# A new layout for the turned attention weights, and earlier quarter sums, in a fused threshold-attention and GELU-MLP kernel

## The chip, the cores and the metric

The kernel runs on one core of one Trainium2 chip. Its time is device microseconds from the first instruction to the last. Five engines work side by side and meet only at semaphores: TensorE (PE in the profile; its weight loads are PEld), VectorE (DVE), ScalarE (ACT), GpSimd (POOL) and SyncE (SP, which here only issues transfers). Sixteen DMA engines move data between HBM and SBUF and within SBUF.

## The reference, cut to what matters

```python
# threshold attention: 8 batches x 8 heads, 576 tokens, head size 64
scores = scale * np.matmul(q, k.transpose(0, 1, 3, 2))
thresh = np.max(scores, axis=-1, keepdims=True) - tau
scores = np.where(scores >= thresh, scores, -1000000000.0)
scores = scores - np.max(scores, axis=-1, keepdims=True)
attn = np.exp(scores)
attn = attn / (np.sum(attn, axis=-1, keepdims=True) + 1e-09)
attn_out = np.matmul(attn, v).astype(np.float32)
# bridge (B,H,S,D) -> (B*S, H*D) = (4608, 512), then the MLP, 512 -> 2048 -> 512
x = np.ascontiguousarray(attn_out.transpose(0, 2, 1, 3)).reshape(B * S, H * D)
h = x @ w_in
g = 0.5 * h * (1.0 + erf(h * inv_sqrt2))      # exact GELU
return (g @ w_out).astype(np.float32)
```

`q`, `k`, `v` are float32; `w_in` and `w_out` arrive as 8-byte floats, which the kernel turns into float32 itself ("conversions" below).

## The kernel before

Two heads make a pair; there are 32 pairs, each in five slots of 128 query rows (the fifth slot holds the 64 left-over rows of both heads). The program is one long list in which every engine's instructions stand in order. Three stages follow one another:

1. **Start** (the first four pairs, some 20 slots). The MLP weights are read and converted; attention weights are turned (queries to the free axis) by TensorE.
2. **Middle** (pairs 4 to 31). The attention weights are turned by VectorE in blocks of 32 x 32, and transfers within SBUF put the blocks in their places (the "regrouping"). TensorE fills the room between with ten of the eighteen MLP blocks of 256 tokens.
3. **End** (the last eight blocks, two at a time, by a Strassen-like scheme with seven products instead of eight). It needs sums and differences of quarters of `w_in` and of the blocks' inputs.

The tiles and the turning, with cuts:

```python
pd = [const.tile([P, 4 * KR, P], FP32, name=f"pd{e}") for e in range(2)]     # P=128, KR=5, Q=32, NB=18
...
def turn_p(p, i):                      # VectorE, in the middle stage: one operation for each head
    w = s.pop(("p", i))
    n = 1 if i == NC else 2
    for e in reversed(range(n)):
        to = pd_tail[p % 2] if i == NC else pd[e][:, :, i * Q:(i + 1) * Q]
        nc.vector.transpose(to[:, 0:NB, :], w[:, e * S:(e + 1) * S].rearrange("p (b i) -> p b i", i=Q))

def regroup(p, i):                     # SyncE issues; i = 1 and 3 move two slots at once, i = NC the tail
    if i == 1:
        s["pT"] = [one.tile([P, KR, S], FP32, tag=f"pT{e}", name=f"pT{e}") for e in range(2)]
    for a in range(4):
        rows = slice(a * Q, (a + 1) * Q)
        if i == NC:
            e, at = divmod(a * Q, TAIL)
            nc.sync.dma_start(s["pT"][e][:, :, MAIN + at:MAIN + at + Q], pd_tail[p % 2][rows])
            continue
        half = slice((i - 1) * Q, (i + 1) * Q)
        for e in (1, 0):
            nc.sync.dma_start(s["pT"][e][:, :, a * P:(a + 1) * P][:, :, half], pd[e][rows, :, half])

def weigh_v(p, lo, hi):                # called twice a pair, with halves of 288 columns
    for c in range(KR):
        for e in range(2):
            nc.tensor.matmul(xT[f, 0:hi - lo], lhsT=s["v"][:, e, c, :], rhs=pT[:, c, lo:hi], ...)
```

A row of `pT` is (5, 576): one matmul reads 288 numbers in a row, and one transfer writes runs of 64 numbers, 256 bytes.

The first loads, and the change from the middle to the end:

```python
def load_early(p):                     # q and k of the first four pairs; v in the same way
    ... src[b, 2 * hp + e, 0:MAIN, :].rearrange("(t p) d -> p t d", p=P)   # runs of 64 numbers
...
elif n == len(slots):
    ext = weights_in()                 # s1, s2, s4: twelve sums of w_in's quarters, on VectorE
...                                    # two slots later: the last pair's weigh_v, then its division
fill(1e12, B * S)                      # what is left of the plain MLP blocks
strassen(*ext)

def strassen(ext, room):
    for h in range(HF // U):
        for c in range(NK):
            a = w_in_sb[c][:, HF + h * U:HF + (h + 1) * U]
            vec.tensor_tensor(a, w_in_sb[c][:, h * U:(h + 1) * U], a, op=ALU.subtract)
    ...
    x_sums(*DUOS[0])                   # four differences of the first two blocks' quarters
    for sb, (n1, n2) in enumerate(DUOS):
        for j in range(NJ):
            product(x, [(lhs_in(c, j, 0), a[:, c, :]) for c in ks], True)
            product(y, [(lhs_in(c, j, 1), b[:, c, :]) for c in ks], True)
            product(x, [(lhs_ext(s2, c, j), t2[:, c, :]) for c in ks])
            ...
        for m in ms:                   # the last products of a duo
            product(xs[m], rows(g12, m, w_out_part(1, 1)))
            nc.scalar.copy(lo[m][:, HD:2 * HD], xs[m])
            row = n1 * TOK + m * P
            nc.sync.dma_start(out[row:row + P, :], lo[m])
```

`lhs_in(c, j, 1)` reads the half of `w_in` that the loop at the head of `strassen` overwrites. `t1`, `t2`, `t4` are what `x_sums` writes.

Of the kernel before, what the change touches and what calls it, by code (L numbers as in the profile page):

```python
# [18 lines left out]
def kernel(  # L19
# [68 lines left out]
    ps = ctx.enter_context(tc.tile_pool(name="ps", bufs=4, space=PSUM))  # L88

    ident = const.tile([P, P], FP32, name="ident")  # L90
    make_identity(nc, ident)
# [3 lines left out]
    v_sb = [const.tile([P, 2, KR, D], FP32, name=f"v{i}") for i in range(4)]  # L95
    pd = [const.tile([P, 4 * KR, P], FP32, name=f"pd{e}") for e in range(2)]
    sums = [const.tile([P, Q], FP32, name=f"sums{i}") for i in range(2)]
# [3 lines left out]
    for t in q_tail + v_sb:  # L101
        nc.gpsimd.memset(t, 0.0)
    for t in pd:
        nc.gpsimd.memset(t[:, NB:4 * KR, :], 0.0)

# [31 lines left out]
    def load_piece():  # L137
        if loaded[0] == len(pieces):
            return
        dst, src = pieces[loaded[0]]  # L140
        loaded[0] += 1
        if not wide:
            nc.sync.dma_start(dst, src)
            converted[0] += 1
            load_piece()
            return
        k = loaded[0] - 1
        if k % 2:

            room = pd[k // 2 % 2][:, 0:NB - 2, :].bitcast(U32).rearrange("p b i -> p (b i)")  # L150
            raw, shifted = room[:, 0:2 * PIECE], room[:, 2 * PIECE:4 * PIECE]
        else:
            raw, shifted = (xg.tile([P, 2 * PIECE], U32, tag="x", name=s) for s in ("raw", "shifted"))
        nc.gpsimd.dma_start(raw, src.bitcast(U32))
        n = 8 * PIECE - 4
        nc.gpsimd.dma_start(shifted.bitcast(U8)[:, 0:n], src.bitcast(U8)[:, 3:3 + n])
        raws.append((dst, raw, shifted))
# [78 lines left out]
    def load_early(p):  # L236
        b, hp = divmod(p, HP)
        s = st[p] = {}
        for name, src in (("q", q), ("k", k)):
            t = s[name] = ld.tile([P, NC + 1, P], FP32, tag=name, name=name)  # L240
            eng = nc.scalar if p < 2 and name == "k" else nc.sync
            for e in range(2):
                eng.dma_start(
                    t[:, 0:NC, e * D:(e + 1) * D],
                    src[b, 2 * hp + e, 0:MAIN, :].rearrange("(t p) d -> p t d", p=P),
                )
            eng.dma_start(
                t[0:TAIL, NC, :].rearrange("p (e d) -> p e d", e=2),
                src[b, 2 * hp:2 * hp + 2, MAIN:S, :].rearrange("e s d -> s e d"),
            )  # L250

    def load_v_early(p):
        b, hp = divmod(p, HP)
        t = st[p]["v"] = v_sb[p % 4]
        for e in range(2):
            nc.sync.dma_start(t[:, e, 0:NC, :], v[b, 2 * hp + e, 0:MAIN, :].rearrange("(t p) d -> p t d", p=P))
            nc.sync.dma_start(t[e * TAIL:(e + 1) * TAIL, e, NC, :], v[b, 2 * hp + e, MAIN:S, :])
# [165 lines left out]
    def turn_p(p, i):  # L423

        s = st[p]
        w = s.pop(("p", i))
        n = 1 if i == NC else 2  # L430
        for e in reversed(range(n)):
            to = pd_tail[p % 2] if i == NC else pd[e][:, :, i * Q:(i + 1) * Q]
            nc.vector.transpose(to[:, 0:NB, :], w[:, e * S:(e + 1) * S].rearrange("p (b i) -> p b i", i=Q))  # L433

    def regroup(p, i):

        s = st[p]
        if i == 1:
            s["pT"] = [one.tile([P, KR, S], FP32, tag=f"pT{e}", name=f"pT{e}") for e in range(2)]
        for a in range(4):  # L440
            rows = slice(a * Q, (a + 1) * Q)
            if i == NC:
                e, at = divmod(a * Q, TAIL)
                nc.sync.dma_start(s["pT"][e][:, :, MAIN + at:MAIN + at + Q], pd_tail[p % 2][rows])
                continue
            half = slice((i - 1) * Q, (i + 1) * Q)
            for e in (1, 0):
                nc.sync.dma_start(s["pT"][e][:, :, a * P:(a + 1) * P][:, :, half], pd[e][rows, :, half])

    def weigh_v(p, lo, hi):  # L450
# [5 lines left out]
        for c in range(KR):  # L456
            for e in range(2):
                f = slice(e * D, (e + 1) * D)
                pT = s["pT"][0 if p < EARLY and c == NC else e]
                nc.tensor.matmul(  # L460
                    xT[f, 0:hi - lo], lhsT=s["v"][:, e, c, :], rhs=pT[:, c, lo:hi],
                    start=(c == 0), stop=(c == KR - 1))
        by = None if p < EARLY else s["inv"]
# [27 lines left out]
    dirty = [False]  # L491
    warm = const.tile([P, 2], FP32, name="warm")
    nc.vector.memset(warm, 0.0)

    def gelus(left):
# [14 lines left out]
    def block_steps(n):  # L510

        g = {}
        for j in range(N_DF):
            if j % 2 == 0:
# [10 lines left out]
        for m in range(TOK // P):  # L525
            for j in range(N_DF):
                yield NS_OUT, len(pieces) - N_DF + j + 1
                if j not in g:
# [9 lines left out]

    mlp = {"n": 0, "steps": None, "next": None, "debt": 0.0}

# [40 lines left out]
    def weights_in():  # L581

        room = [x for tag in ("q", "k", "qT", "kT") for _ in range(2) for x in unit(ld, tag)]
        room += unit(work, "p", 2) + unit(work, "p", 2)
        rest = [units(v_sb[i % 4])[0] for i in range(NP - 4, NP - 1)]
        s1, s2, s4 = ({} for _ in range(3))
        for h in range(HF // U):
            lo, hi = slice(h * U, (h + 1) * U), slice(HF + h * U, HF + (h + 1) * U)
            for c in range(NK):
# [4 lines left out]
                vec.tensor_tensor(s4[c, h], w_in_sb[NK + c][:, lo], s2[c, h], op=ALU.subtract)  # L594
        return (s1, s2, s4), room + rest

# [9 lines left out]

    def strassen(ext, room):
        s1, s2, s4 = ext
        for h in range(HF // U):
            for c in range(NK):  # L610
                a = w_in_sb[c][:, HF + h * U:HF + (h + 1) * U]
                vec.tensor_tensor(a, w_in_sb[c][:, h * U:(h + 1) * U], a, op=ALU.subtract)
        room = room + units(v_sb[(NP - 1) % 4]) + [u for t in pd_tail for u in units(t)]
        room += [x for _ in range(2) for x in unit(xg, "x", 2)]
        x_ext = [room.pop().rearrange("p (c t) -> p c t", c=NK) for _ in range(3)]
        o_ext = [room.pop() for _ in range(2)]
        room += [x for _ in range(N_DF // 2 + 2) for x in unit(gp, "g")]
        room += [u for t in pd for u in units(t)]
        for e in range(2):
# [28 lines left out]

        def x_sums(n1, n2):
            t1, t2, t4 = x_ext  # L650
            a, b = x_blk[n1], x_blk[n2]
            b11, b21, b12, b22 = a[:, 0:NK, :], a[:, NK:2 * NK, :], b[:, 0:NK, :], b[:, NK:2 * NK, :]
            vec.tensor_tensor(t1, b12, b11, op=ALU.subtract)
            vec.tensor_tensor(t2, b22, t1, op=ALU.subtract)
            vec.tensor_tensor(b12, b22, b12, op=ALU.subtract)  # L655
            vec.tensor_tensor(t4, b21, t2, op=ALU.subtract)

        def w_out_sums(j):
# [5 lines left out]
            vec.tensor_tensor(wt4(j), b21, wt2(j), op=ALU.subtract)  # L664

        def finish_chunk(j, x, p3):
            product(x, p3)
# [4 lines left out]

        x_sums(*DUOS[0])
        for sb, (n1, n2) in enumerate(DUOS):
# [45 lines left out]
            for m in ms:  # L720
                xs[m] = bank("sc")[:, 0:HD]
                product(xs[m], rows(g11, m, w_out_part(0, 0)), True)
                nc.scalar.copy(lo[m][:, 0:HD], xs[m])
                vec.tensor_tensor(lo[m][:, 0:HD], lo[m][:, 0:HD], vs[m], op=ALU.add)
            for n in DUOS[sb + 1] if sb + 1 < len(DUOS) else ():
                if n in away:
                    bring(n)
            if sb + 1 < len(DUOS):
                x_sums(*DUOS[sb + 1])
            for m in ms:  # L730
# [6 lines left out]
            for m in ms:  # L737
                product(ys[m], rows(g22, m, wt4))
                vec.tensor_tensor(hi[m][:, 0:HD], hi[m][:, 0:HD], ys[m], op=ALU.add)
            for m in ms:  # L740
                product(xs[m], rows(gs1, m, wt1))
                vec.tensor_tensor(hi[m][:, HD:2 * HD], hi[m][:, HD:2 * HD], xs[m], op=ALU.add)
                row = n2 * TOK + m * P
                nc.sync.dma_start(out[row:row + P, :], hi[m])
            for m in ms:
                product(xs[m], rows(g12, m, w_out_part(1, 1)))
                nc.scalar.copy(lo[m][:, HD:2 * HD], xs[m])
                row = n1 * TOK + m * P
                nc.sync.dma_start(out[row:row + P, :], lo[m])

    load_early(0)
    load_early(1)
    for _ in range(2):
# [8 lines left out]
    for g, (chunks, pairs) in enumerate(parts):  # L762
        first = 0 if g < 2 else HP + g - 2
        slots += [(p, i) for p in range(first, first + pairs) for i in chunks]
    BATCH = HP * SLOTS
    WEIGH = 2
    START = 2 * HP + 2
# [17 lines left out]
    for n in range(len(slots) + WEIGH + 1):  # L785
# [15 lines left out]
        if p > EARLY and i == WEIGH:  # L801
            made = [weigh_v(p - 1, h * HALF, (h + 1) * HALF) for h in range(2)]
        owed += (goal(n) - goal(n - 1)) * BLK_NS * (PARTS[i] if not early and p < NP else 1.0)
# [33 lines left out]
        if n == BATCH:  # L837
            for t in pd_tail:
                nc.gpsimd.memset(t[:, NB:4 * KR, :], 0.0)
# [61 lines left out]
```

## Time and profile before

| | value |
|---|---|
| time, median of 3 runs (lowest, highest) | 1428.99 us (1428.49, 1430.3) |
| profiled span | 1430.0 us |
| TensorE busy / weight loads busy | 1385.1 / 960.9 us |
| VectorE / ScalarE / GpSimd busy | 900.0 / 640.8 / 389.1 us |
| packets on the queues of SyncE (q1) | 423184, of 449492 in all |
| `pT<-pd` transfers | 448 of 160 KB, median 3.9 us to landing |
| VectorE turning, `pd<-p` 128x576 | 224 of 756 ns, 160.8 us |

How to read it: busy time is the union of an engine's instructions, and matmuls are pipelined, so a busy TensorE isn't TensorE at its peak; the distance from one matmul's start to the next one's says more. An engine that is not the limit costs nothing while it waits. In the waits view, "A <- B: total, times, longest" says that A sat idle until B had finished. In the timeline a row is start, length, engine, line, operation, names, count, with the idle time before it in brackets. `o_ps`, `hT` are the plain MLP, `bank` the end stage, `sc` the scores, `xT` the product with `v`, `tr` TensorE's turning.

### The profile page before, as it was taken

The numbers are of one execution on the slowest core, as the hardware profiler recorded it, in microseconds if no ns is written. First come the engines' busy times: TensorE is split into PE (matmuls) and PEld (weight loads), VectorE is DVE, ScalarE is ACT, GpSimd is POOL, SyncE is SP. The second block draws the span as 40 slices with busy tenths as digits, with TensorE's granted clock in tenths as the row PEclk, the third lists the DMA queues.
The fourth block names the chain that finished last, engine by engine and source line by source line (L and its number), as shares of the span: only waits on it lengthen the run. The fifth ranks groups of instructions, "written<-read, shape, count | busy, mean of one in ns | idle before, by whom it ended". The sixth has DMA issues, their size and how long they took to land.

```text
span 1430.0 us, 19776 instructions
## 1 busy us (share of the span) xinstructions
PE 1385.1 (97%) x6544; PEld 960.9 (67%) x6544; DVE 900.0 (63%) x1908; ACT 640.8 (45%) x1039; POOL 389.1 (27%) x810
## 2 busy tenths in 40 slices
PE   5898999999999999999999999999999999999999
PEld 4666547566466574665746657466488888888887
DVE  5887787777767777777777777777654142241230
ACT  5758525436256373562745627457142141230320
POOL 4443244433434434434434344330000000000000
PEclk8999999999999999999999999999999999999999
DMA  9977167776667776677776777765500100100000
GB/s 260 297 264 241 40 144 150 152 150 133 131 137 145 153 147 133 142 140 159 156 140 143 160 154 152 142 135 100 107 0 1 44 1 0 59 1 8 22 1 30
DMA packets 449492, 167.06 MB, mean 117 GB/s; under 512 B 413040, under 2 KB 432048, under 8 KB 449392
## 3 DMA queue, kind: packets, MB, share of 16 engines
q1 hardware_dynamic: 423184, 108.65, 38.8%
q0 software_dynamic: 23808, 56.57, 12.9%
q8 instruction: 53, 0.87, 0.2%
q10 hardware_dynamic: 2400, 0.59, 0.2%
q14 instruction: 47, 0.39, 0.1%
HBM read 71.68 MB, written 11.47 MB: 58 GB/s over the span
## 4 chain that ended last, share of the span: by engine, by line
PE 85%; DVE 6%; ACT 5%; DMA 2%; issue 1%; SPq 1%; POOL 0%; DVEq 0%; ACTq 0%; POOLq 0%
PE bank L641 27%; PE hT L520 18%; PE o_ps L532 17%; PE sc L355 12%; PE xT L460 9%; ACT p L370 2%; DVE p L386 1%; PE tr L301 1%; DVE nmx L367 1%; DVE power L185 1%; ACT L500 1%; ACT diag L400 1%; DMA pd<-in_moe_w_in_dram 1%; ACT L507 0%; DVE expo L176 0%
## 5 line engine op out<-in xcount | busy, mean ns | idle before, releaser
L370 ACT ACTIVATE p<-sc,nmx 128x576 f32<-128x576 f32 x288 | 202.5, 739 | 384.4 <-DVE nmx L367 384.4
L367 DVE TENSOR_REDUCE nmx<-sc 128x1 f32<-128x576 f32 x288 | 205.0, 749 | 149.8 <-PE sc L355 149.8
L520 PE MATMUL hT<-x,w_in 128*128 128x256 f32 x1280 | 296.2, 384 | 0.0
L532 PE MATMUL o_ps<-w_out,g 128*128 128x512 f32 x640 | 295.1, 604 | 0.0
L520 PEld LDWEIGHTS hT<-x,w_in 128*128 128x128 f32 x1280 | 238.4, 190 | 56.9 <-issue 25.2
L386 DVE SCALAR_TENSOR_TENSOR p<-sc,thr,p 128x576 f32<-128x576 f32 x288 | 225.4, 816 | 65.2 <-ACT p L370 64.2
L368 POOL TENSOR_SCALAR thr<-nmx,tau_eff 128x1 f32<-128x1 f32 x288 | 85.0, 295 | 547.4 <-DVE nmx L367 544.9
L532 PEld LDWEIGHTS o_ps<-w_out,g 128*128 128x128 f32 x640 | 117.1, 190 | 141.0 <-issue 139.2
L355 PE MATMUL sc<-kT,qT 64*128 64x288 f32 x960 | 165.0, 432 | 2.6 <-DVE p L386 2.4
L460 PE MATMUL xT<-pT,v 128*64 128x288 f32 (+2 forms) x1280 | 164.4, 409 | 3.2 <-ACT g L500 3.2
L433 DVE STREAM_TRANSPOSE pd<-p 128x576 f32<-128x576 f32 x224 | 160.8, 756 | 2.9
L355 PEld LDWEIGHTS sc<-kT,qT 64*128 64x128 f32 x960 | 92.9, 187 | 84.2 <-issue 71.8
L460 PEld LDWEIGHTS xT<-pT,v 128*64 128x64 f32 x1280 | 90.2, 137 | 73.4 <-issue 13.5
L232 POOL DMA_DIRECT2D v<-in_v_dram x208 | 111.0, 537 | 10.5 <-issue 9.5
L641 PE MATMUL bank<-x,w_in 128*128 128x256 f32 x384 | 94.7, 383 | 3.2 <-DVE x L655 3.2
L507 ACT ACT_TABLE_LOAD x71 | 91.1, 1283 | 1.3
L500 ACT ACT_TABLE_LOAD x71 | 91.1, 1283 | 1.3
L641 PE MATMUL bank<-unit 128*128 128x256 f32 x352 | 88.6, 382 | 0.0
L641 PEld LDWEIGHTS bank<-x,w_in 128*128 128x128 f32 x384 | 73.7, 192 | 14.2 <-issue 4.1
L223 POOL DMA_DIRECT2D q<-in_q_dram x104 | 70.9, 686 | 15.9 <-issue 15.0
L641 PEld LDWEIGHTS bank<-unit 128*128 128x128 f32 x352 | 67.4, 192 | 9.4
L301 PE MATMUL tr<-diag,p 128*128 128x128 f32 (+1 forms) x360 | 51.8, 312 | 22.1 <-ACT diag L400 13.8
(143 smaller groups left out, 1346.4 us busy)
## 6 DMA issues: line engine op xcount, KB each, us to landing
pT<-pd SPq DMA_DIRECT2D x448, 160.0 KB, 3.9
pT<-pd_tail SPq DMA_DIRECT2D x112, 80.0 KB, 2.8
q<-in_q_dram POOLq DMA_DIRECT2D x104, 72.0 KB, 4.0
k<-in_k_dram POOLq DMA_DIRECT2D x104, 72.0 KB, 2.6
out_dram<-o_sb SPq DMA_DIRECT2D x28, 256.0 KB, 3.9
inv<-turned SPq DMA_DIRECT2D x56, 128.0 KB, 3.9
v<-in_v_dram POOLq DMA_DIRECT2D x156, 40.0 KB, 3.0
raw<-in_moe_w_in_dram POOLq DMA_DIRECT2D x8, 512.0 KB, 5.5
```

The source lines that it names most:

```text
L232: eng.dma_start(t[r:P:4, e, 0:n, :], rows[:, r * KR:r * KR + n, :])
L355: nc.tensor.matmul(sc[e][:, h, 0:HALF], lhsT=lhsT, rhs=s["kT"][rows, at:at + HALF], start=True, stop=True)
L367: nc.vector.tensor_reduce(nmx[:, e:e + 1], sc, axis=AXIS.XY, op=ALU.max, negate=True)
L370: nc.scalar.activation(w[:, e * S:(e + 1) * S].rearrange("p (h s) -> p h s", h=2), sc, AF.Exp, bias=nmx[:, e:e + 1], scale=1.0)
L386: nc.vector.scalar_tensor_tensor(row, sc[e][:, :, 0:HALF], thr[:, e:e + 1], row, op0=ALU.is_ge, op1=ALU.mult, accum_out=den[e])
L433: nc.vector.transpose(to[:, 0:NB, :], w[:, e * S:(e + 1) * S].rearrange("p (b i) -> p b i", i=Q))
L460: nc.tensor.matmul(xT[f, 0:hi - lo], lhsT=s["v"][:, e, c, :], rhs=pT[:, c, lo:hi], start=(c == 0), stop=(c == KR - 1))
L500: nc.scalar.activation(t, hT, AF.Gelu)
L507: nc.scalar.activation(warm[:, 1:2], warm[:, 0:1], AF.Exp)
L520: nc.tensor.matmul(hT[:, j % 2, :], lhsT=w_in_sb[c][:, j * P:(j + 1) * P], rhs=x_blk[n][:, c, :], start=(c == 0), stop=(c == N_DM - 1))
L532: nc.tensor.matmul(o[:, 0:d_model], lhsT=g[j][:, m * P:(m + 1) * P], rhs=w_out_sb[j], start=(j == 0), stop=(j == N_DF - 1))
L641: nc.tensor.matmul(to, lhsT=l, rhs=r, start=start and k == 0, stop=k == len(pairs) - 1, skip_group_check=not start)
```

## The change

**Turned weights.** One tile `turned_p` of shape (2 heads, 2 halves, 20, 64) for each partition takes the place of the two `pd`. One VectorE operation turns both heads of a slot. `pT` is read as (9 groups of 64 queries, 5, 64), so that one regrouping transfer writes 128 runs of 5 x 64 numbers, 1280 bytes. The product with `v` then reads its columns as groups of 64, 320 numbers apart, and is split in 320 and 256 columns instead of 288 and 288.

**End stage.** The differences within `w_in` and the first `x_sums` are put behind the last slot, into `weights_in`, two slots ahead of the last division. Each output row block is stored in two halves, each as soon as it is complete.

**Start.** `k` and `v` of the first four pairs are read with four rows of HBM next to each other in a partition (runs of 1024 bytes); `q` stays as it was. A first Exp on a dummy tile stands behind the first loads. The zeros in the padding of the turned weights are written when the middle stage begins, no longer at the very start.

```diff
-    pd = [const.tile([P, 4 * KR, P], FP32, name=f"pd{e}") for e in range(2)]
+    turned_p = const.tile([P, 2, 2, 4 * KR, 2 * Q], FP32, name="turned_p")
+    pd = [turned_p[:, e, :, :, :].rearrange("p h b i -> p (h b i)") for e in range(2)]
...
-    for t in pd:
-        nc.gpsimd.memset(t[:, NB:4 * KR, :], 0.0)
...
+                order = "(t p) d -> p t d" if name == "q" else "(p t) d -> p t d"
                 eng.dma_start(
+                    t[:, 0:NC, e * D:(e + 1) * D], src[b, 2 * hp + e, 0:MAIN, :].rearrange(order, p=P))
...   # turn_p
-        for e in reversed(range(n)):
-            to = pd_tail[p % 2] if i == NC else pd[e][:, :, i * Q:(i + 1) * Q]
-            nc.vector.transpose(to[:, 0:NB, :], w[:, e * S:(e + 1) * S].rearrange("p (b i) -> p b i", i=Q))
+        nc.vector.transpose(
+            turned_p[:, :, i // 2, 0:NB, i % 2 * Q:(i % 2 + 1) * Q], w.rearrange("p (e b i) -> p e b i", e=2, i=Q))
+
+    def by_64(t):
+        return t.rearrange("p c s -> p (c s)").rearrange("p (g c s) -> p g c s", c=KR, s=2 * Q)
...   # regroup
-                nc.sync.dma_start(s["pT"][e][:, :, a * P:(a + 1) * P][:, :, half], pd[e][rows, :, half])
+                nc.sync.dma_start(by_64(s["pT"][e])[:, 2 * a + h, :, :], turned_p[rows, e, h, :, :])
...   # weigh_v
+                    to = to.rearrange("p (g s) -> p g s", s=2 * Q)
+                    rhs = by_64(s["pT"][e])[:, lo // (2 * Q):hi // (2 * Q), c, :]
...   # weights_in, behind the twelve sums
+        for h in range(HF // U):
             for c in range(NK):
                 a = w_in_sb[c][:, HF + h * U:HF + (h + 1) * U]
                 vec.tensor_tensor(a, w_in_sb[c][:, h * U:(h + 1) * U], a, op=ALU.subtract)
+        x_sums(x_ext, *DUOS[0])
...   # strassen
-        x_sums(*DUOS[0])
...
+                store(n2, m, hi[m], 0)
...
-                row = n1 * TOK + m * P
-                nc.sync.dma_start(out[row:row + P, :], lo[m])
+                store(n1, m, lo[m], HD)
...
     load_early(0)
+    nc.scalar.activation(warm[:, 1:2], warm[:, 0:1], AF.Exp)
     load_early(1)
...
+    WIDE = 5 * 2 * Q
...
-            made = [weigh_v(p - 1, h * HALF, (h + 1) * HALF) for h in range(2)]
+            made = [weigh_v(p - 1, lo, hi) for lo, hi in ((0, WIDE), (WIDE, S))]
...
-            for t in pd_tail:
+            for t in pd_tail + [turned_p[:, e, h, :, :] for e in range(2) for h in range(2)]:
                 nc.gpsimd.memset(t[:, NB:4 * KR, :], 0.0)
```

## The prediction, made before the changed kernel ran

> **What bounds the kernel now.** I read the busy shares by slice first, then a table of the stages, then TensorE's own waits, and last the timeline around the one long wait late in the run.
>
> ```profile
> PE 1385.1 (97%) x6544; PEld 960.9 (67%) x6544; DVE 900.0 (63%) x1908; ACT 640.8 (45%) x1039; POOL 389.1 (27%) x810
> ...
> PEclk8999999999999999999999999999999999999999
> ```
>
> TensorE is busy almost everywhere. The stage table says where it isn't; its columns are the window, its length, each engine's busy us with counts, granted clock, DMA share, GB/s.
>
> ```profile
> 0.00:200.00 200.00, 168.40 (x932) 116.99 (x932) 150.67 (x335) 127.26 (x235) 77.54 (x168) 0.93 0.73 213
> 200.00:1000.00 800.00, 795.37 (x3711) 487.90 (x3712) 605.14 (x1239) 408.94 (x542) 310.64 (x639) 1.00 0.71 143
> 1000.00:1040.00 40.00, 36.77 (x131) 19.19 (x128) 23.08 (x44) 5.70 (x9) 0.88 (x3) 0.92 0.48 95
> 1040.00:1430.00 390.00, 384.58 (x1777) 336.86 (x1775) 121.10 (x292) 98.88 (x254) 0.00 (x0) 1.00 0.04 15
> ```
>
> In the 800 us of the middle TensorE lacks 4.6 us, at full clock. VectorE (76%) and the DMA engines (71%) have room there. So the start lacks 31.6 us, the passage to the end stage 3.2 us, the end 5.4 us. That no slack hides in this busy time I took from the distances of starts in the trace: between 200 and 1015 us the plain MLP's matmuls of 256 columns start a median 216 ns apart, the same as in the end stage, where nothing else runs.
>
> ```profile
> PE tr L301 <- ACT diag L400: 13.8, 7, 5.6
> PE tr L275 <- DMA q<-in_q_dram: 6.5, 1, 6.5
> ...
> PE xT L460 <- ACT g L500: 3.2, 2, 1.6
> PE bank L641 <- DVE x L655: 3.2, 1, 3.2
> ...
> PE sc L355 <- DVE p L386: 2.4, 7, 1.0
> ...
> PE tr L283 <- DMA q<-in_q_dram: 1.8, 1, 1.8
> ```
>
> No wait for `pT`, for a regrouping or for the turning (L433) is in TensorE's list. What the change is named for is off the path; its side parts touch the waits that exist.
>
> ```profile
> 1029.13 0.95 DVE L478 TENSOR_TENSOR x<-xT,inv 128x64 f32<-128x64 f32 x4 [5.30 <-DMA inv<-turned]
> ...
> 1030.00 2.49 DVE L612 TENSOR_TENSOR w_in<-w_in 128x512 f32<-128x512 f32 x4
> ...
> 1030.31 1.03 PE L641 MATMUL bank<-x,w_in 128*128 128x256 f32 x4
> ...
> 1033.73 0.68 DVE L655 TENSOR_TENSOR x<-x 128x512 f32<-128x512 f32 x1
> ...
> 1034.57 2.04 PE L641 MATMUL bank<-x,w_in 128*128 128x256 f32 x4 [3.23 <-DVE x L655]
> ...
> 1036.40 1.91 PE L641 MATMUL bank<-unit 128*128 128x256 f32 x4
> ...
> 1040.89 1.03 PE L641 MATMUL bank<-unit 128*128 128x256 f32 x4
> ```
>
> Here the first product of the end stage runs at 1030.31, and the second waits until VectorE, itself held 5.30 us by `inv`, has divided, differenced `w_in` and made the first `x_sums`. The same four matmuls then take 2.04 us instead of 1.03: half clock, until 1040.
>
> **What the skill says.** (1) "TensorE: Matmul & The Clock Gate", part 1, the HAM clock gate: an idle window of about 3.4 us puts the array at half clock, and a busy one brings it back. The trace agrees: 3.23 us idle, then some 5.3 us with starts 427 ns apart instead of 216. (2) "VectorE: DVE Perf Modes", the errata section: an fp32 tensor_tensor takes (N+151)/0.96 ns; at N=576 that is 757, and the turning measures 756 here, so I use it for the merged one. (3) "DMA: Bandwidth & Descriptors", why small descriptors are slow: it says that transfers within SBUF suffer little. The trace's packets of 256 bytes from HBM in the start took 18 ns each, of 4096 bytes 159 ns or more: 14 against 26 bytes per ns. (4) "Advanced Engine Details and Errata", SBUF cachelines: full rate needs consecutive accesses in one 16-byte line. Runs of 64 floats meet that. No run so far shows a matmul with such a stepped operand.
>
> **The change, part by part.**
>
> *Turning.* 28 pairs x 4 slots x 2 = 224 operations of 756 ns become 112 of (1152+151)/0.96 = 1357 ns (estimate): 112 x (1512 - 1357) = 17 us of VectorE. TensorE's waits on VectorE in the middle are the seven of `sc <- p L386`, 2.4 us. I grant 0.7 us.
>
> *Regrouping.* 448 transfers go from 640 runs of 256 bytes to 128 of 1280: some 230,000 of 423,184 packets vanish. TensorE waits for none, so this is 0 us on the path. SyncE's issue of one (median 0.9 us) may shorten too, also hidden.
>
> *Product with v.* 320 + 256 columns are the 576 of before, in as many instructions: 0 us, if the stepped operand costs nothing.
>
> *Passage.* VectorE's list behind the last slot: the twelve sums end at 1023.83; then four differences (2.5 us) and four `x_sums` (4 x 0.69 = 2.7 us) end near 1029.0, inside the 5.30 us in which it waited for `inv` anyway. The second product needs nothing later, so TensorE goes on at 1031.2. Removed: a start distance of 3.61 us instead of 0.22, so 3.4 us; and 13 matmuls at half clock, with the first of them slow too, 2.8 us. Together **6.2 us**; I count 5.9, for a bank that might come free late.
>
> *Start.* The first wait, 6.49 us, ends with the first `q`; up to 7 us about 3,650 packets of 256 bytes went by in the trace's packet records, 2,170 of them `k` on ScalarE's queue. As a quarter as many of 1024 bytes, at an estimated 48 ns (between 18 for 256 and 159 for 4096), `k` takes 1.6 instead of 2.4 us of the sixteen engines, and the Exp's table load (1.28 us) delays the second `k` behind it: 0.7 us gained. The table load itself, at 6.42 us, hid behind TensorE's turning of `k`, so it's worth some 0.1 more. From 10 to 60 us the DMA engines are full, and the conversions wait for them; VectorE serves conversions and attention in one order, so that the 5.6 us wait at 22.35 us goes back to weights that landed at 20.8 us. `k` and `v` of the four pairs are 8 x 1,024 = 8,192 packets; 2,048 of those are the first two `k`. The other 6,144 cost 6,144 x 18 / 16 = 6.9 us of the engines, and 1,536 x 48 / 16 = 4.6 us in the new form: 2.3 us, of which I take 1.7 to reach TensorE. GpSimd issues the first weights 0.56 us earlier without its two zero fills; those were converted without a wait, so 0. The 200 us of the start lose 7% of the clock, 14 us, beside 31.6 us idle; with 2.5 us less idle I count 0.5 less of it. Sum of the start **3.0 us**. TensorE is saturated from 200 us on, so what the start gains arrives at the end whole.
>
> *Tail.* The last transfer is 128 KB instead of 256 KB; at the 26 bytes per ns and engine of above that is 0.3 us less.
>
> Sum: 0.7 + 5.9 + 3.0 + 0.3 = 9.9 us, 1428.99 - 9.9 = **1419 us**.
>
> **Rivals.** *A: the stepped operand slows the product with v.* xT takes 5.0 us a pair (a timeline row of 40 such instructions is 5.07 us long), 28 x 5.0 = 140 us in all. A quarter slower would be +35 us: 1454. For it speaks only that no such operand has been seen here; against it, point (4). I give 4%. *B: the start eats its gain.* Its waits pass between `diag`, gelu and DMA (5.0 us on L500 alone), and the 93% clock there shifts with each gap; in-order lists can catch the gain at the next gelu. Then only passage and tail remain: 1422. *C: the other way, the start gains more than traffic:* fewer gaps, so less half clock; of the 14 us of clock loss some 3 us more could come back, and some of the 5.6 us wait: 1415. *D: the passage's wait moves,* for the last division or a free bank: 2 to 3 us given back, 1422.
>
> **Range and chances.** B and D pull up by 3 us each, C down by 3 or 4; from 1419 this makes 1412 to 1424.5. Faster by over 2% would need 28.6 us, nearly all that the start loses: 2%. Slower by over 2% is rival A alone: 4%. The rest, 94%, is within 2%.
>
> **What would show each step.** Right: no wait of TensorE of over 1 us near 1030 us, and the four-matmul rows there at 1.03 us; a first matmul at about 5.7 us; turning operations of 1152 columns near 1357 ns; q1 packets near 190,000; middle windows with busy and starts as before. Wrong: xT starts over 240 ns apart for each two instructions (rival A); a start stage with over 31 us idle (B); the half clock back at the passage (D).

## The result, and the profile after

| | before | after |
|---|---|---|
| time, median (lowest, highest) | 1429.19 (1428.49, 1430.3) | 1422.57 us (1420.38, 1423.59) |
| ratio, 95% interval | | 0.9951 (0.9934 to 0.9968) |
| profiled span | 1430.0 | 1421.8 us |

The change saves about 7 us, 0.5%: within the 2% band, inside the predicted range, 3.6 us above the predicted time. The same changed kernel was timed a second time among the experiments (-6.1 us). The two profiles that are compared below lie 8.2 us apart: the profile of the kernel before is of an execution of 1432.1 us, slower than the four timed ones, so the differences between the two profiles are somewhat larger than those between medians.

First the page of the changed kernel: busy times, packets, and the groups that the change touches.

```profile
PE 1382.1 (97%) x6544; PEld 958.8 (67%) x6544; DVE 892.6 (63%) x1788; ACT 640.9 (45%) x1040; POOL 388.0 (27%) x812
...
DMA packets 219347, 167.05 MB, mean 117 GB/s; under 512 B 122480, under 2 KB 203952, under 8 KB 219248
...
q1 hardware_dynamic: 193040, 108.65, 36.2%
...
q10 hardware_dynamic: 2400, 0.59, 0.2%
...
L473 PE MATMUL xT<-pT,v 128*64 128x256 f32 (+1 forms) x1280 | 163.7, 409 | 2.7 <-ACT g L509 2.7
L434 DVE STREAM_TRANSPOSE turned_p<-p 128x1152 f32<-128x1152 f32 x112 | 154.1, 1376 | 3.0
```

SyncE's queue q1 lost 230,144 packets, as counted. The merged turning takes 1376 ns; 1357 was the estimate. The product with `v` keeps its busy time (164.4 us before). In q10, ScalarE's queue with the first `k`, the 2400 packets are the same number as before: the transfers that were to be made of fewer, longer packets were not.

The stage table after, with the same windows and columns:

```profile
0.00:200.00 200.00, 169.73 (x934) 117.39 (x936) 150.66 (x330) 127.47 (x236) 77.94 (x170) 0.94 0.71 214
200.00:1000.00 800.00, 795.71 (x3718) 488.23 (x3718) 598.99 (x1128) 408.88 (x542) 309.22 (x639) 1.00 0.66 143
1000.00:1040.00 40.00, 40.00 (x159) 23.32 (x155) 26.42 (x51) 9.23 (x18) 0.87 (x3) 1.00 0.45 95
```

The last window is full now, at full clock, where 3.2 us were missing. The middle has 0.3 us more TensorE time, and its DMA share fell from 0.71 to 0.66. The start has 1.3 us less idle time, but only 0.4 us of it shows in the starts of matching instructions (below).

TensorE's own waits after:

```profile
PE tr L302 <- ACT diag L401: 11.4, 7, 2.8
PE tr L276 <- DMA q<-in_q_dram: 9.5, 2, 6.3
PE tr L302 <- ACT g L509: 5.0, 4, 2.3
PE xT L473 <- ACT g L509: 2.7, 2, 1.3
PE sc L356 <- DVE p L387: 2.5, 6, 0.9
```

The wait of the end stage for `x` (3.2 us) is gone. In the start a second wait for loads has come: two waits of 9.5 us together where one of 6.5 stood, while the longest wait for `diag` halved from 5.6 to 2.8. One has largely replaced the other.

The timeline of the changed kernel at the passage:

```profile
1022.69 2.49 DVE L611 TENSOR_TENSOR w_in<-w_in 128x512 f32<-128x512 f32 x4
...
1027.02 0.69 DVE L632 TENSOR_TENSOR v<-x,v 128x512 f32<-128x512 f32 x1
...
1027.63 0.88 DVE L490 TENSOR_TENSOR x<-xT,inv 128x64 f32<-128x64 f32 x3
...
1028.63 1.89 PE L663 MATMUL bank<-x,w_in 128*128 128x256 f32 x8
...
1030.36 1.03 PE L663 MATMUL bank<-v,unit 128*128 128x256 f32 x4
...
1032.94 1.03 PE L663 MATMUL bank<-v,unit 128*128 128x256 f32 x4
```

The differences and `x_sums` are done at 1027.7, and the division (L490) follows them without a wait for `inv`; the first two products are one row of eight matmuls, with no wait between them and no half clock behind.

**Where the 8.2 us came from.** I subtracted the starts of matching instructions in the two profiles. By 166 us the changed kernel leads by 0.4. The lead falls to 0.16 near 224 us, then grows to 1.06 by 1005 us, in three steps of 0.26 to 0.37 us (two of them shorter waits of `xT` for a gelu). The last pair's product with `v` takes 5.00 us instead of 5.62, which brings the lead to 1.68. From there to the product at 1032.94 (1040.89 before) it jumps to 7.95: 6.27 us for the passage. From the end of the last copy to the end of the span it is 2.71 instead of 3.00 us: 0.29. The sum is 8.2.

### The profile page after: what moved, and what is told of

Same layout as the page of the kernel before. It is cut to its first block, busy times and chain, and to the rows that moved or that the text cites. A ratio compares the mean times of both kernels' runs of the same rounds, so it can differ in the third digit from the quotient of the medians.

```text
span 1421.8 us, 19662 instructions
## 1 busy us (share of the span) xinstructions
PE 1382.1 (97%) x6544; PEld 958.8 (67%) x6544; DVE 892.6 (63%) x1788; ACT 640.9 (45%) x1040; POOL 388.0 (27%) x812
## 4 chain that ended last, share of the span: by engine, by line
PE 87%; DVE 5%; ACT 5%; DMA 2%; issue 1%; SPq 0%; POOL 0%; DVEq 0%; ACTq 0%; POOLq 0%
PE bank L663 27%; PE o_ps L543 18%; PE hT L530 18%; PE sc L356 12%; PE xT L473 10%; ACT p L371 1%; DVE p L387 1%; PE tr L302 1%; DVE power L187 1%; DMA q<-in_q_dram 1%; DVE nmx L368 1%; ACT L509 1%; ACT diag L401 1%; DMA turned_p<-in_moe_w_in_dram 1%; ACT power L179 0%
## 5 line engine op out<-in xcount | busy, mean ns | idle before, releaser
L473 PE MATMUL xT<-pT,v 128*64 128x256 f32 (+1 forms) x1280 | 163.7, 409 | 2.7 <-ACT g L509 2.7
L434 DVE STREAM_TRANSPOSE turned_p<-p 128x1152 f32<-128x1152 f32 x112 | 154.1, 1376 | 3.0
L663 PE MATMUL bank<-w_out,unit 128*128 128x256 f32 x416 | 92.4, 379 | 0.0
L663 PEld LDWEIGHTS bank<-w_out,unit 128*128 128x128 f32 x416 | 79.0, 190 | 10.7
L302 PE MATMUL tr<-diag,p 128*128 128x128 f32 (+1 forms) x360 | 51.4, 311 | 19.6 <-ACT diag L401 11.4
```

The lines of the kernel that those rows point to most:

```text
L434: nc.vector.transpose(turned_p[:, :, i // 2, 0:NB, i % 2 * Q:(i % 2 + 1) * Q], w.rearrange("p (e b i) -> p e b i", e=2, i=Q))
L473: nc.tensor.matmul(to, lhsT=s["v"][:, e, c, :], rhs=rhs, start=(c == 0), stop=(c == KR - 1))
L663: nc.tensor.matmul(to, lhsT=l, rhs=r, start=start and k == 0, stop=k == len(pairs) - 1, skip_group_check=not start)
```

## The experiments

The ratio is always to the kernel before on the same chip, with its 95% interval; 0.001 is 1.43 us. My theory was that of the prediction, with the passage as the main part; the rivals were that the layout, or the start, brought the gain.

**Only the passage** (the kernel before, with the differences and first `x_sums` behind the last slot):

```diff
+        for h in range(HF // U):        # in weights_in, behind the twelve sums
+            ...
+                vec.tensor_tensor(a, w_in_sb[c][:, h * U:(h + 1) * U], a, op=ALU.subtract)
+        x_sums(x_ext, *DUOS[0])
```

> The kernel before with one part alone: the differences within w_in and the first x_sums stand behind the last slot. Theory (the gain is the passage): TensorE's 3.2 us wait and the half clock behind it go, -5 to -6.3 us, which is nearly the whole of the change's -6.6. Rival (the layout gains): about -3 or less, since VectorE would still be late for the end stage. Rows of four products near 1035 us take 1.03 us under the theory, 2.04 us under the rival.

Measured: 1423.4 us, ratio 0.9966 (0.9953 to 0.9979), so -4.9 us (-3.0 to -6.7). TensorE's timeline of this kernel at the passage:

```profile
1031.88 1.89 PE L654 MATMUL bank<-x,w_in 128*128 128x256 f32 x8
1033.60 1.03 PE L654 MATMUL bank<-v,unit 128*128 128x256 f32 x4
```

The wait and the half clock go, as in the changed kernel, without any of the layout. This part alone is most of the gain (about two thirds by the medians; the interval allows more and less).

**Only the layout** (the kernel before with `turned_p` at the address of the old `pd`, one turning for both heads, runs of 1280 bytes, columns split 320 + 256, and the later zero fills):

```diff
-                nc.sync.dma_start(s["pT"][e][:, :, a * P:(a + 1) * P][:, :, half], pd[e][rows, :, half])
+                nc.sync.dma_start(by_64(s["pT"][e])[:, 2 * a + h, :, :], turned_p[rows, e, h, :, :])
```

> The kernel before with the layout alone: one turning operation per slot, runs of 1280 bytes, the product with v in 320 and 256 columns, zero fills at the start of the middle stage; the differences stay where they were. Theory (the layout is off the path): -0.3 to -1.5 us, out of a few waits of the middle and the last pair's tail, and the 3.2 us wait at the end stage stays. Rival (the layout gains): -3 us or more. In both the transfers on SyncE's queue fall from 423184 packets to near 194000.

Measured: 1427.98 us, ratio 0.999 (0.998 to 1.0001): -1.4 us, and zero is just inside. TensorE at the passage:

```profile
1034.36 1.10 PE L652 MATMUL bank<-x,w_in 128*128 128x256 f32 x4 [2.44 <-DVE x L666]
...
1036.90 1.91 PE L652 MATMUL bank<-unit,w_in 128*128 128x256 f32 x4
```

The wait for `x` stays, 2.44 us long, and is again followed by half clock (1.91 us where 1.03 is full speed). What the change is named for does not remove it.

**Only the start** (the kernel before with the new order of `k` and `v`, the dummy Exp, the later zero fills; the dummy's tile is declared ahead of the other constants, as in the changed kernel):

```diff
+    warm = const.tile([P, 2], FP32, name="warm")      # moved to the front of the constants
...
+                order = "(t p) d -> p t d" if name == "q" else "(p t) d -> p t d"
...
+    nc.scalar.activation(warm[:, 1:2], warm[:, 0:1], AF.Exp)
```

> The kernel before with the start's parts alone: k and v of the first four pairs with four rows of HBM next to each other, the dummy Exp between the first two loads, zero fills later. Theory (the Exp delays the second pair's k, and k is still written in 256-byte runs): -0.5 to +0.5 us; packets of ScalarE's queue stay 256 bytes long, and TensorE waits about 3 us for the second pair's k near 15 us. Rival (the start gains as predicted): -2 to -3 us.

Measured: 1434.44 us, ratio 1.0035 (1.0023 to 1.0047): 5.0 us *slower*. Both expectations of the time were wrong. Most of the loss is not in the start: between the same two score matmuls, which before's profile begins at 206 and 953 us, 750.8 us pass here and 747.4 before. VectorE's timeline in the middle of this kernel shows where some of that arises:

```profile
703.06 0.52 DVE L477 TENSOR_TENSOR x<-xT,inv 128x192 f32<-128x192 f32 x2 [5.68 <-DMA inv<-turned]
```

VectorE waits 5.68 us for a division's `inv`, and TensorE's waits for `p` rise from 2.4 to 4.6 us in all. Something 500 us after the start had been disturbed by a change of the start. Two experiments below follow this up, a third asks the same of the new layout.

**All but the passage** (the changed kernel with the differences and `x_sums` back in `strassen`):

```diff
-                vec.tensor_tensor(a, w_in_sb[c][:, h * U:(h + 1) * U], a, op=ALU.subtract)   # in weights_in
-        x_sums(x_ext, *DUOS[0])
+        x_sums(*DUOS[0])                                                                   # in strassen
```

> The changed kernel with the differences and the first x_sums back at the head of the end stage. Theory (the gain is the passage): near the kernel before, -0.5 to -2 us, with the wait of about 3 us and the half clock back. Rival (the layout gains): -3.5 us or more.

Measured: 1426.91 us, ratio 0.9991 (0.9982 to 1.0001). TensorE at the passage:

```profile
1030.44 1.10 PE L650 MATMUL bank<-x,w_in 128*128 128x256 f32 x4 [2.54 <-DVE x L664]
1031.38 1.03 PE L650 MATMUL bank<-unit 128*128 128x256 f32 x4
```

Taking the passage out of the changed kernel gives back 0.9991 - 0.9951 = 0.4% (0.2 to 0.6), 5.7 us; from both sides it is the main part. The row also shows something about the clock: a wait of 2.54 us, and *no* half clock behind it, while 2.44 us in the layout kernel had it. The Trainium skill ("TensorE: Matmul & The Clock Gate", part 1) says the activity window runs freely, so it matters where in it the idle time falls. The records of the granted clock agree: its changes within a run lie whole multiples of 3.41 us apart. I cut the profiles into stretches of 3.41 us at these changes. The wait of the layout kernel then lies almost whole in one stretch; that of the start kernel, 3.30 us long, lies half in one and half in the next. The windows view of TensorE (stretch, length, busy time, granted clock, DMA share, GB/s), the layout kernel, then the start kernel:

```profile
1031.98:1035.40 3.42, 1.04 (x5) 1.00 0.20 77
1035.40:1038.81 3.41, 3.41 (x10) 0.50 0.02 5
```

```profile
1034.56:1037.97 3.41, 1.78 (x7) 1.00 0.21 77
1037.97:1041.38 3.41, 1.74 (x8) 1.00 0.02 5
1041.38:1044.79 3.41, 3.41 (x18) 1.00 0.00 0
```

Half clock follows the shorter wait and not the longer one. I counted this in all fourteen profiles, for the stretches at full clock later than 60 us: each of the 27 with 1.95 us or more in which no matmul ran was followed by half clock, and of some 5,500 that were not, none had more than 1.92 us. (In the first 60 us half clock also came behind 1.4 to 1.8 us.) The prediction took an idle window of about 3.4 us from that page as what it takes; here 2 us within one such stretch were enough, and the measurement decides. So the half clock's 2.8 us belong to some executions only: before's profile has two such stretches behind the wait (6.83 us), three profiles of kernels that keep the wait have one, two have none. This fits the 4.9 us of the timed runs being less than the 6.27 between the two profiles.

**The constants 32 bytes higher** (the kernel before; only the declaration of the small tile `warm` moves from its old place to the front of the constants, so that `pd` starts at 160 instead of 128 modulo 256, and the other constant tiles move by 32 bytes too):

```diff
+    warm = const.tile([P, 2], FP32, name="warm")      # ahead of pd
+    nc.vector.memset(warm, 0.0)
...
-    warm = const.tile([P, 2], FP32, name="warm")      # its old place, behind them
-    nc.vector.memset(warm, 0.0)
```

> The kernel before with nothing but that shift: the small tile is declared first, so that all constants behind it lie 32 bytes higher. Theory (the shift): SyncE's mean issue of a regrouping rises from 894 to about 957 ns, packets of 256 bytes from 22 to 24 ns, and the time by 2 to 5 us. Rival (not the shift): within 1 us of the kernel before, issues near 895 ns.

Measured: 1433.9 us, ratio 1.0032 (1.0022 to 1.0042): 4.5 us for nothing but addresses. No instruction differs but the place of one tiny fill. The tiles view of the regrouping (issuing time min/median/max, first and last start) of the kernel before, then of this one:

```profile
L448 SPq DMA_DIRECT2D pT<-pd x448: 609/906/1897, 176.8 to 1016.7; - x150
```

```profile
L450 SPq DMA_DIRECT2D pT<-pd x448: 609/1014/1873, 172.8 to 1016.5; - x150
```

One issue takes 0.11 us longer in the median (0.07 in the mean), and a transfer lands after 4.1 instead of 3.9 us. SyncE issues in order, and `turned` and `inv` (the sums' way through a transfer to the division) stand behind the regrouping in its list. What VectorE's division waits for, from the groups of the kernel before and then of this one:

```profile
L478 DVE TENSOR_TENSOR x<-xT,inv 128x192 f32<-128x192 f32 (+7 forms) x112 | 28.9, 300 | 14.0 <-DMA inv<-turned 7.5 <-PE xT L460 3.7 <-issue 1.7
```

```profile
L480 DVE TENSOR_TENSOR x<-xT,inv 128x192 f32<-128x192 f32 (+7 forms) x112 | 28.5, 295 | 33.6 <-DMA inv<-turned 31.2 <-issue 1.5 <-PE xT L462 0.2
```

7.5 us of waiting for `inv` became 31.2. And it reaches TensorE: the stretch that took 747.4 us before takes 751.0, the middle window has less busy time than before's 795.4 us, with a DMA share of 0.75 instead of 0.71, and the waits for `p` doubled from 2.4 to 5.1.

```profile
200.00:1000.00 800.00, 792.61 (x3701) 485.98 (x3701) 601.80 (x1235) 407.25 (x540) 309.77 (x637) 1.00 0.75 143
```

```profile
PE sc L357 <- DVE p L388: 5.1, 11, 1.0
```

**The start again, without the shift** (the start kernel above, with the small tile put where it moves no constant):

```diff
-    warm = const.tile([P, 2], FP32, name="warm")
+    warm = small.tile([P, 2], FP32, tag="warm", name="warm", bufs=1)
```

> The start's parts alone, as in the third run, which was 5 us slower than the kernel before and lost 3.4 us of it in the middle, behind late inv tiles. There the dummy Exp's small tile stood first in SBUF, so that pd and the other constants lay 32 bytes higher; here it stands elsewhere, and pd and pT have the addresses of the kernel before. Theory (the shift makes the regrouping's 256-byte packets slower, so that SyncE's list and the inv tiles behind it run late): SyncE's mean issue of a regrouping falls from 957 to about 895 ns, the 5.7 us wait for inv near 703 us is gone, and the time is within 2 us of the kernel before. Rival (a part of the start itself disturbs the middle): still 4 to 6 us slower, with late inv tiles.

Measured: 1430.98 us, ratio 1.0009 (0.9999 to 1.0018); the waits for `inv` are back to 9.2 us, an issue to a median of 912 ns, and the stretch of the middle to 747.4 us. So of the start kernel's +5.0 us the shift was most, and the parts of the start by themselves bring +1.3 us (-0.1 to +2.6): not the predicted gain of 3.0.

**The Exp later** (the changed kernel, dummy Exp behind the second group of loads):

```diff
     load_early(0)
-    nc.scalar.activation(warm[:, 1:2], warm[:, 0:1], AF.Exp)
     load_early(1)
+    nc.scalar.activation(warm[:, 1:2], warm[:, 0:1], AF.Exp)
```

> The changed kernel with the dummy Exp behind the second pair's loads instead of before them. Theory (the table load delays the second pair's k, which then stands behind the first weights in the DMA engines): TensorE's 3.2 us wait near 15.7 us shrinks to about 1.8 us or less, k of the second pair has landed by about 8 us, and the start comes out 0.5 to 1.5 us shorter. Rival (the start is held by VectorE's list and the conversions whatever k does): the wait moves to the next one, and the time stays within 0.4 us of the changed kernel.

Measured: 1421.46 us, ratio 0.9937 (0.9924 to 0.9951). ScalarE's timeline of the *changed* kernel shows what the early Exp does:

```profile
2.78 1.28 ACT L768 ACT_TABLE_LOAD   x1 [2.78 <-issue]
3.47 0.56 ACTq L246 DMA_DIRECT2D k<-in_k_dram  x1
...
5.50 0.55 ACTq L246 DMA_DIRECT2D k<-in_k_dram  x1
```

The second pair's `k` went out together from 2.53 us before; now, behind the start of the table load, the halves go at 3.47 and 5.50, and the 512 packets of the second move between 10.0 and 14.8 us, among the first weights, where before they were through by 7.2. TensorE turns this `k` at 15.73 us (12.56 before). With the Exp later it is 14.61:

```profile
13.73 1.08 PE L276 MATMUL tr<-ident,q 128*128 128x128 f32 x4 [2.39 <-DMA q<-in_q_dram]
14.61 1.06 PE L276 MATMUL tr<-ident,k 128*128 128x128 f32 x4
```

The 3.2 us wait for this `k` is gone, but TensorE now waits 2.4 us for the same pair's `q`: the wait has moved, as the rival said, and shrunk a little. The pair's scores begin at 15.98 us (16.71 in the changed kernel, 15.25 before). The time may be 1 us better than the changed kernel's; the intervals overlap, so that stays open.

**`k` in long packets at last.** (the changed kernel; `k` stored head by head in SBUF too, and turned by plain matmuls with the identity, 64 columns each):

```diff
-                eng.dma_start(
-                    t[:, 0:NC, e * D:(e + 1) * D], src[b, 2 * hp + e, 0:MAIN, :].rearrange(order, p=P))
+                to = t[:, 0:NC, e * D:(e + 1) * D] if name == "q" else by_head(t)[:, e, :, :]
+                eng.dma_start(to, src[b, 2 * hp + e, 0:MAIN, :].rearrange(order, p=P))
...
+                for e in range(2):
+                    nc.tensor.matmul(tr[e * D:(e + 1) * D, c, :], lhsT=by_head(t)[:, e, c, :], rhs=ident, start=True, stop=True)
```

> The changed kernel with the first four pairs' k stored head by head in SBUF, so that both ends of the transfer have runs of 1024 bytes; TensorE turns k in two matmuls of 64 columns a chunk instead of one of 128. Theory (my prediction counted runs at the HBM end alone): packets of 256 bytes on ScalarE's queue go down by about 2,000 (1024-byte ones come in), and the first k costs less; if traffic were the limit of the start, 1 to 2 us shorter. Rival (the start is held by the order of work, not by traffic): within 0.5 us of the changed kernel.

Measured: 1423.5 us, ratio 0.9952 (0.9939 to 0.9965), the changed kernel's. The queue of ScalarE in this kernel:

```profile
q10 hardware_dynamic: 864, 0.59, 0.2%
```

864 packets instead of 2400: now the runs are 1024 bytes long (512 of the packets; the rest are tails). In the changed kernel they were not, because its `k` tile holds two heads side by side and each transfer fills one of them, 64 numbers at steps of 128: a packet was as long as the shorter of the runs at its two ends. With the long packets the first `q` is there at 6.10 us (6.26), but TensorE still waits 1.97 and 0.76 us for the second `k`, and its turning takes longer (1.97 instead of 1.06 us a pair). Fewer packets for `k` were not worth the predicted time.

**Both together** (long packets, and the Exp later, the two edits above):

> The changed kernel with both: k head by head in runs of 1024 bytes, and the dummy Exp behind the second loads. If traffic and the late k are the limits of the start, 1.5 to 3 us shorter than the changed kernel, the start I had predicted, and faster than both kernels. If the order of work holds it, within 0.5 us of it.

Measured: 1425.8 us, ratio 0.997 (0.9958 to 0.9982), slower than with the later Exp alone. TensorE's start in this kernel:

```profile
5.71 1.08 PE L280 MATMUL tr<-ident,q 128*128 128x128 f32 x4 [5.71 <-DMA q<-in_q_dram]
...
10.68 0.27 PE L291 MATMUL tr<-ident,q 64*128 64x64 f32 x1 [1.98 <-DMA q<-in_q_dram]
...
15.94 1.09 PE L280 MATMUL tr<-ident,q 128*128 128x128 f32 x4 [2.56 <-DMA q<-in_q_dram]
```

The first matmul is at 5.71 us, the very figure that was predicted for the change, and nothing comes of it: two new waits for later loads follow. By the medians neither expectation holds: it is 3.2 us slower than the changed kernel, though the two intervals overlap a little. For `k`, then, less traffic did not make the start shorter; that the order of the loads and of the engines' lists holds it instead is what these timelines suggest, not more.

**The moving operand by single numbers** (the changed kernel; the product with `v` reads numbers 5 apart instead of groups of 64, so it multiplies other weights; instructions and columns are as many):

```diff
-                    rhs = by_64(s["pT"][e])[:, lo // (2 * Q):hi // (2 * Q), c, :]
+                    rhs = flat.rearrange("p (s c) -> p c s", c=KR)[:, c, lo:hi]
```

> The changed kernel with the product with v reading single numbers 5 apart instead of runs of 64 that are 320 apart (so it multiplies other weights than the reference does; the number of columns and everything else is as in the changed kernel). It asks where a stepped operand begins to cost. If each number's own 16-byte line costs, the starts of two such instructions lie far more than the 263 ns (320 columns) and 210 ns (256) of the changed kernel apart, say 1.5 to 2 times, and the whole is 60 to 140 us longer. If the step is free at fp32's rate, they stay at 263 and 210 ns and the time within 2 us.

Measured: 1571.19 us, ratio 1.0988 (1.0971 to 1.1005), some 148 us above the changed kernel. A pair's forty instructions in the timeline of the changed kernel, then of this one:

```profile
600.46 5.07 PE L473 MATMUL xT<-pT,v 128*64 128x320 f32 x40
```

```profile
599.64 10.48 PE L473 MATMUL xT<-pT,v 128*64 128x320 f32 x40
```

5.07 us is what the plain rows took before; 10.48 is 2.1 times as much, and 28 pairs of 5.4 us are 151. So the operand's pattern can cost, and groups of 64 do not.

**The Exp later and the constants at multiples of 256 bytes** (the later Exp, and a filler that puts `turned_p` at 0 instead of 160 modulo 256):

```diff
-    warm = const.tile([P, 2], FP32, name="warm")
+    warm = const.tile([P, 32], FP32, name="warm")
```

> The changed kernel with the dummy Exp behind the second pair's loads and its tile widened to 128 bytes, so that turned_p and the other constants begin at multiples of 256 bytes. With runs of 1280 bytes I expect no late inv tile to be left to save: the same as with the late Exp alone, 0.5 to 2 us faster than the changed kernel, if the late Exp's gain is real; if run-to-run changes of the start made it, within 0.7 us.

Measured: 1421.45 us, ratio 0.9946 (0.9934 to 0.9958). A packet of 1280 bytes takes 87 ns instead of 96 in the mean, the DMA share of the middle falls to 0.61, and the time is as with the later Exp. In the new layout the address made no difference to the time that could be seen.

**The changed kernel again,** beside the last three:

> The changed kernel again, beside the others of this group, as their measure: 1421 to 1424 us, -5 to -8 us against the kernel before.

Measured: 1423.34 us, ratio 0.9957 (0.9944 to 0.997). The two kernels with the later Exp and `k` as in the change, at 1421.5 us, are the fastest seen and beat the kernel before clearly; against the changed kernel they can't be told apart.

## Why the prediction was right or wrong

**Passage: right in its steps, high in its size.** 6.2 us were worked out and 5.9 counted; the two profiles give 6.27, by the steps that were named: no wait, four-matmul rows at 1.03 us. But that is no second measurement, because the 6.2 was read from the same profile of the kernel before, and there the half clock was at its longest. From the first to the 25th matmul of the end stage the six profiles with the old order take 8.0 to 11.4 us (before: 11.4), those with the new order 5.2: a gain of 2.8 to 6.3 us, 4.6 in the mean. Timed alone it is -4.9 us (-3.0 to -6.7). Rival D did not come.

**Start: wrong.** "Sum of the start 3.0 us" is the step that failed; the profiles show 0.4, and the start's parts alone, without the shift, cost 1.3 us (-0.1 to +2.6). Its first term fell at once: `k` stays in 256-byte packets, since I had counted the runs at the HBM end only; the first matmul came at 6.26 us (6.49 before), not at the predicted 5.7. The table load, which I expected to help by delaying the second `k`, delayed it into the weights' traffic, and a wait of 3.2 us there stands against the 2.8 us gained on `diag`. The term of 1.7 us, traffic converted into time, falls for `k` with the long-packet runs: a quarter of the packets for its main rows, and no better time. For `v`, whose packets did become 1024 bytes (48 ns in the median, as estimated, 58 in the mean), it wasn't tried alone. Rival B described this: the start eats its gain, total 1422 (its sign, over 31 us idle in the start, was missed by little: 30.3). A pair of profiles can't settle the start: the matmul that before's profile begins at 206 us comes 1.0 us later and 4.0 us earlier in two others with before's start code, and 0.5 and 2.2 us earlier and 0.3 later in three with the changed kernel's. The timed runs of the start alone decide.

**Regrouping 0: right, but only just.** With the old addresses it was off the path: the layout alone is worth -1.4 us, zero included. But "off the path" had little slack. The 32 bytes that the change itself adds cost the old layout 4.5 us (3.1 to 6.0); in the new one no such cost was seen. Its line in the tiles view:

```profile
L456 SPq DMA_DIRECT2D pT<-turned_p x448: 542/612/1907, 177.0 to 1015.0; - x150
```

An issue of 128 runs holds SyncE 612 ns in the median, where 640 runs held it 906, and VectorE's waits for `inv` in the middle are gone. So I had missed that the regrouping is one list away from the path, and that the change shifts the constants. That the shift slows the old layout is shown; *why* is open. The Trainium skill ("DMA: Bandwidth & Descriptors", how a descriptor splits into AXI transactions) says that a run which does not start at a multiple of 256 bytes makes the engine fetch from the multiple below. With its unit of 32 bytes a 256-byte run is 12 such units at 128 and 13 at 160 (my estimate from that page). Packets in the middle did go from 21.8 to 23.5 ns in the mean, but the median stayed at 18: the slow packets became slower, not each one, which such a unit more for every packet does not explain by itself. Other effects of the addresses aren't excluded.

**Middle: 0.7 predicted,** and 0.66 in the profile up to 1005 us, though from waits for gelu, not for `p`; the last pair's quicker product adds 0.6. **Product with `v`: 0,** as measured; rival A is out. The Trainium skill's rule on SBUF cachelines ("Advanced Engine Details and Errata") put both cases on the right side, and the 2.1 gives it a size. **Tail: 0.3,** 0.29 measured.

In the sum, the parts timed alone give -4.9 (passage), -1.4 (layout) and +1.3 us (start), -5.0 together and -5.3 with the tail, where the whole gives -7.0 (-4.6 to -9.4) and, measured again, -6.1: they add up within the intervals. Of the 9.9 us predicted, the start's 3.0 are missing and about one of the passage's; the layout gave a little more than its 0.7 by the profiles. That the median of 1422.6 us is what rivals B and D gave speaks for B alone; D's figure is met by luck.

## What to carry to other kernels

Look for the gain at the wait that ends last, not at the part a change is named for: here eight subtractions, moved ahead, made about two thirds of it. A cost that was read from one profile, as the half clock was here, may be an extreme: look at a second one. Count the runs of a transfer at both its ends before counting packets. A queue that no one on the path waits for can still be one in-order list away from it; measure its slack, and when a small tile moves, ask which larger ones move with it.

## What the runs showed of the hardware that was not expected

- Constants 32 bytes higher made 448 transfers within SBUF issue in 1014 instead of 906 ns and the kernel 4.5 us slower.
- A wait of 2.44 us was followed by half clock, one of 3.30 us at the same place was not: with the profile cut into stretches of 3.41 us at the clock's changes, 1.95 us or more without a matmul in one stretch brought half clock in 27 of 27 cases later than 60 us, and none came behind stretches with less than 1.9.
- A matmul's moving operand in single floats 5 apart takes 2.1 times as long as in groups of 64 floats, which cost nothing.
